# Linear attention and two feed-forwards: converting the second down projection's rows in the second feed-forward

## The chip, the cores and the metric

The program runs on one core of one Trainium2 chip. The metric is the device time of one execution in microseconds. A core has five engines that run their own instruction queues and wait for each other by semaphores: TensorE (PE: matmuls; PEld: its weight loads), VectorE (DVE), ScalarE (ACT), GpSimd (POOL) and SyncE (SP), which here issues nearly all DMAs.

## The reference

```python
def _attn_ref(q, k, v, g_norm):            # 4 x 8 heads x 576 x 64
    kv = np.einsum('bhsd,bhse->bhde', k, v)
    out = np.einsum('bhsd,bhde->bhse', q, kv)
    rms = np.sqrt(np.mean(out * out, axis=-1, keepdims=True) + 1e-06)
    return out / rms * g_norm
def _moe_ref(x, w_gate, w_val, w_out):     # 2304 x 512, d_ff 1536
    g = x @ w_gate
    return (g / (1 + np.exp(-g)) * (x @ w_val)) @ w_out
def _moe2_ref(x, w_in, w_out):             # d_ff 2048
    h = x @ w_in
    return (np.maximum(h, 0) + np.log1p(np.exp(-np.abs(h)))) @ w_out
```

The three are chained: `_moe2_ref(_moe_ref(_attn_ref(...)))`. The weights come as 64-bit floats, all else as 32-bit floats.

## The kernel before

**Precision.** Every operand of a feed-forward matmul is split into a high part in the fast 32-bit form (fp32r, a cast on ScalarE) and a low part (the difference, on GpSimd or VectorE); `mm3` makes three matmuls of a product: high x high, and the two mixed ones. A weight tile of 128 x 512 arrives as 64-bit floats and is converted by bit operations (`convert`): a scaled copy on ScalarE (L260), a shift and two merges on VectorE (L263, L264, L268). Then come the high part on ScalarE and the low part.

**Tokens.** The 2304 tokens are four tiles of 512 (t = 0 to 3) and one of 256 (t = 4, "B"). The first feed-forward loops over the 12 column blocks j of d_ff, and in each over the five tiles: gate and value products (pg, pv), silu and product on ScalarE and VectorE (s, u, split into uh and ul), and the down product py, which VectorE adds into yacc (L493). py is made of two units' tails woven into later units, and its PSUM tiles are three (pool `po`).

**The second feed-forward** makes its up products in 7 instead of 8 block products (a Strassen-like scheme): two column blocks of w2_in (a "pair", jp = 0 to 7) against two token tiles. A block of seven products, `quad`, has the steps p1, p5, p6, p2, p7, p3, p4 on the banks X, Y and Z; between them stand the down products pz of the pair before (`late`), which VectorE adds into zacc (L779). Products and sums become the tiles c11, c22, c12, c21; ScalarE makes their softplus and the high part gh (L679, L680), GpSimd the low part gl (L681). The first pass (n = 0) takes token tiles 0 and 1 through all eight pairs, the second (n = 1) tiles 2 and 3, with the small tile B woven in (`rest`).

**Its operands** are made ahead. In the first feed-forward `pair2` converts a pair of w2_in column blocks (zi), makes four sums of them (s, L551) and the two row blocks of w2_out (zp), splits all six into kh and kl, and writes them to DRAM (w2d); `load2` brings them back, once in each pass. For the tokens, `block_steps` makes seven blocks b of yacc and of sums of yacc (L622), each with a high half on ScalarE (L605) and a low half (L609) on the engine that `BLO` names: for the first pass in the last turn j = 11 (`blocks1`), for the second in the last block of the first pass (`blocks2`).

**The order** is written out by the program itself: TensorE's steps are emitted in a fixed order, each advances a nominal clock by 0.216 us a matmul of 512 columns, and `defer(dt, f)` puts all other work into a heap that is emptied as that clock passes. STEP2 is the distance of a pair's steps on it, PAIR2 that of the pairs. Each engine runs what it got in the order in which it was emitted; tiles come from pools of a fixed number of buffers, and a tile waits for the last reader of the buffer that it takes over. The pool `stage` (5 buffers) holds raw weights and the first two column tiles wh of a pair.

Of the kernel before, what the change touches and what calls it, by code (L numbers as in the profile page):

```python
# [68 lines left out]
def tile_linear_attention_two_ffn(  # L69
# [411 lines left out]
    def ffn1_o(j, t):  # L481
        w = widths[t]

        def step(d):
# [15 lines left out]
            if j == F1 - 1 and t == B:  # L500
                if d == 0:
                    x_tiles(t, "y")
                defer(ADD1, part)
# [112 lines left out]

    def t_sum(n, o, a, b):
        def f():  # L620
# [4 lines left out]
    def half(n, i):
        return lambda: halves(n)[i]

    def block_steps(n, tags):

        return [  # L630
            block(n, 0, tags[0], half(n, 0)),
            t_sum(n, 0, 2, 0) + block(n, 1, tags[1], half(n, 0)),
            t_sum(n, 0, 3, 0) + block(n, 2, tags[2], half(n, 0)),
            block(n, 3, tags[3], half(n, 1)),
            t_sum(n, 2, 3, 2) + block(n, 4, tags[4], half(n, 2)),
            block(n, 5, tags[5], half(n, 3)),
            t_sum(n, 1, 1, 0) + block(n, 6, tags[6], half(n, 1)),
        ]
# [4 lines left out]
    def spread(steps, at, every):  # L643
        return [(at + every * i, f) for i, f in enumerate(steps)]

    def blocks1(t):

        if t == 1:
            s = block_steps(0, TAGS1)
            blk["steps"] = s  # L650
            return spread(s[0] + s[3], 0.5, 1.0)
        s = blk["steps"]
# [8 lines left out]
    def blocks2():
        s = block_steps(1, TAGS2)
        r = spread(s[0], 0.2, 0.6)
        for i in range(1, 7):
            r += spread(s[i], 1.4 + 2.4 * (i - 1), 0.75)
        return r
# [320 lines left out]
```

## Time and profile before

| | |
|---|---|
| median of 3 runs | 936.11 us (934.92 to 938.82) |
| profiled execution | 934.92 us, span 933.1 us |
| granted clock, mean over the span | 0.992 |
| PE, PEld busy | 890.3 us (95%), 741.4 us (79%) |
| DVE, ACT, POOL busy | 557.0, 335.6, 253.8 us (60, 36, 27%) |
| moved by DMA | 130.8 MB, mean 140 GB/s |

In the trace, attention and the first two turns of the first feed-forward take until about 150 us, the other turns until about 546 us, the first pass of the second feed-forward until about 700 us, the second pass until about 906 us, and then come the last down products and stores. A row of a timeline gives the start, the duration, the engine, the line and the instruction with the tile written <- tiles read; in brackets stands how long the engine was idle before it, and what ended that. Matmuls overlap: a busy TensorE has a matmul of 512 columns begin every 0.227 us.

### The profile page before, as it was taken

What the parts mean: (1) busy time and instruction counts of PE and PEld (TensorE: products, weight loads), DVE (VectorE), ACT (ScalarE), POOL (GpSimd) and SP (SyncE); (2) the same over time, 40 slices, a digit from 0 to 9 for tenths busy, and PEclk for the clock granted to TensorE, in tenths of its full rate; (3) what the DMA queues carried; (4) which work ended last, traced back from release to release, by engine and by line L of the source; (5) the groups of instructions that cost most, each with busy time, mean ns of one, the idle gap of its engine ahead of it and who ended that gap; (6) DMA issues with size and microseconds to landing.
All of it is one profiled execution on the core that took longest, in us unless ns stands there. A gap on an engine that the chain in (4) does not pass through costs nothing.

```text
span 933.1 us, 11802 instructions
## 1 busy us (share of the span) xinstructions
PE 890.3 (95%) x4352; PEld 741.4 (79%) x4352; DVE 557.0 (60%) x874; ACT 335.6 (36%) x586; POOL 253.8 (27%) x197
## 2 busy tenths in 40 slices
PE   6889999999999999999999889999999999999994
PEld 5668888888888878888778778888877888888883
DVE  3955457988888778888896653333365333333332
ACT  3634434433334333333341352333344333332330
POOL 1633211414133222323131342222222322222220
PEclk9999999999999999999999999999999999999997
DMA  9975202344473636453536041544333543333102
GB/s 276 243 133 116 91 1 91 131 162 154 140 225 106 234 115 221 136 182 136 181 113 225 22 158 35 182 172 154 135 136 136 181 181 136 136 136 136 46 12 101
DMA packets 95453, 130.79 MB, mean 140 GB/s; under 512 B 28836, under 2 KB 57508, under 8 KB 95140
## 3 DMA queue, kind: packets, MB, share of 16 engines
q1 hardware_dynamic: 95236, 130.05, 42.8%
q8 instruction: 34, 0.56, 0.3%
q14 instruction: 23, 0.19, 0.1%
q10 hardware_dynamic: 160, 0.00, 0.0%
HBM read 100.14 MB, written 29.88 MB: 139 GB/s over the span
## 4 chain that ended last, share of the span: by engine, by line
PE 74%; DVE 18%; ACT 3%; issue 2%; DMA 1%; POOL 0%; SPq 0%; DVEq 0%; ACTq 0%; POOLq 0%
PE pz L433 20%; PE py L433 11%; PE pg L433 11%; PE pv L433 10%; PE hY L433 8%; PE hZ L433 4%; DVE yacc L493 4%; PE hX L433 2%; PE hr L433 2%; DVE ul L476 1%; DVE s L551 1%; ACT uh L475 1%; DVE u L472 1%; PE pa L363 1%; PE kvp L315 1%
## 5 line engine op out<-in xcount | busy, mean ns | idle before, releaser
L779 DVE TENSOR_TENSOR zacc<-zacc,pz 128x512 f32<-128x512 f32 x126 | 86.4, 687 | 160.5 <-PE pz L433 160.5
L433 PE MATMUL pz<-wo,gh 128*128 128x512 f32 x576 | 178.0, 390 | 1.1 <-ACT c L679 1.1
L493 DVE TENSOR_TENSOR yacc<-yacc,py 128x512 f32<-128x512 f32 (+1 forms) x220 | 133.3, 626 | 24.9 <-PE py L433 24.6
L681 POOL TENSOR_TENSOR gl<-c,gh 128x512 fp32r<-128x512 f32 x64 | 82.6, 1293 | 234.0 <-ACT gh L680 191.4
L433 PEld LDWEIGHTS pz<-wo,gh 128*128 128x128 f32 x576 | 106.8, 188 | 22.4 <-ACT c L679 1.5
L433 PE MATMUL pz<-wo,gl 128*128 128x512 f32 x288 | 112.3, 390 | 0.3 <-POOL gl L681 0.3
L433 PE MATMUL py<-uh,oh 128*128 128x512 f32 (+1 forms) x240 | 91.3, 380 | 11.3 <-DVE yacc L493 9.5
L433 PE MATMUL hY<-b,wh 128*128 128x512 f32 x384 | 97.6, 390 | 1.2 <-DVE c L709 1.2
L475 ACT CAST uh<-u 128x512 fp32r<-128x512 f32 (+1 forms) x60 | 34.7, 578 | 158.0 <-DVE u L472 157.9
L433 PE MATMUL pv<-xh,vh 128*128 128x512 f32 (+1 forms) x240 | 90.1, 376 | 0.0
L433 PE MATMUL pg<-xh,gh 128*128 128x512 f32 (+1 forms) x240 | 90.0, 375 | 0.0
L433 PE MATMUL pg<-xl,gh 128*128 128x512 f32 (+1 forms) x240 | 88.6, 369 | 0.5 <-DVE xl L401 0.5
L433 PE MATMUL py<-ul,oh 128*128 128x512 f32 (+1 forms) x240 | 88.6, 369 | 0.3 <-DVE ul L476 0.3
L433 PE MATMUL pv<-xh,vl 128*128 128x512 f32 (+1 forms) x240 | 88.8, 370 | 0.0
L433 PE MATMUL py<-uh,ol 128*128 128x512 f32 (+1 forms) x240 | 88.7, 370 | 0.0
L433 PE MATMUL pv<-xl,vh 128*128 128x512 f32 (+1 forms) x240 | 88.6, 369 | 0.0
L433 PE MATMUL pg<-xh,gl 128*128 128x512 f32 (+1 forms) x240 | 88.5, 369 | 0.0
L433 PEld LDWEIGHTS hY<-b,wh 128*128 128x128 f32 x384 | 71.6, 188 | 16.2 <-DVE c L709 1.7
L476 DVE TENSOR_TENSOR ul<-u,uh 128x512 fp32r<-128x512 f32 (+1 forms) x60 | 43.9, 732 | 39.2 <-ACT uh L475 39.2
L433 PEld LDWEIGHTS py<-uh,oh 128*128 128x128 f32 x240 | 45.2, 188 | 24.6 <-DVE yacc L493 15.1
L433 PEld LDWEIGHTS pz<-wo,gl 128*128 128x128 f32 x288 | 54.1, 188 | 12.6 <-POOL gl L681 1.2
L679 ACT ACTIVATE c<-c 128x512 f32<-128x512 f32 x48 | 30.3, 632 | 87.8 <-DVE c L709 87.7
(109 smaller groups left out, 1481.2 us busy)
## 6 DMA issues: line engine op xcount, KB each, us to landing
wh<-w2d SPq DMA_DIRECT2D x32, 512.0 KB, 6.5
wh<-w2d SPq DMA_DIRECT2D x64, 256.0 KB, 7.1
wo<-w2d SPq DMA_DIRECT2D x64, 256.0 KB, 3.7
w2d<-kh SPq DMA_DIRECT2D x48, 256.0 KB, 2.3
w2d<-kl SPq DMA_DIRECT2D x48, 256.0 KB, 2.4
ir<-in_moe_w_in_dram SPq DMA_DIRECT2D x16, 512.0 KB, 5.6
pr<-in_moe_w_out_dram SPq DMA_DIRECT2D x16, 512.0 KB, 3.8
gr<-in_moe_w_gate_dram SPq DMA_DIRECT2D x12, 512.0 KB, 4.5
```

Source lines behind the costliest of these rows:

```text
L315: nc.tensor.matmul(pk[:, hp, :], lhsT=kt[:, c, i:i + 2, :].rearrange("p h d -> p (h d)"), rhs=vt[:, i:i + 2, c * D:(c + 1) * D], start=(c ...
L363: nc.tensor.matmul(pv[p0:p0 + n, hp, :], lhsT=qt[:, hp, p0:p0 + n], rhs=kvm[bb][:, hp, :], start=True, stop=True,)
L433: nc.tensor.matmul(dst, lhsT=a, rhs=b_, start=first and i == 0, stop=last and i == n - 1, skip_group_check=not check)
L472: nc.vector.tensor_mul(u, s[0], pv)
L475: nc.scalar.copy(uh, u)
L476: (nc.gpsimd if UL1 == "g" else nc.vector).tensor_sub(ul, u, f32(uh))
L493: defer(ADD1, lambda: nc.vector.tensor_add(a[:, d, :], a[:, d, :], p))
L551: (nc.vector.tensor_sub if op == "-" else nc.vector.tensor_add)(o, a, b)
L679: nc.scalar.activation(l, src, AF.Softplus)
L681: nc.gpsimd.tensor_sub(lo, l, f32(hi))
L779: defer(ADD2, lambda: nc.vector.tensor_add(av[:, m, :], av[:, m, :], p))
```

## The change

- The row blocks of w2_out are no longer converted in the first feed-forward, nor written to DRAM and loaded twice. `load_rows2` loads the two raw row blocks of a pair into `stage` tiles, and `rows2` converts and splits them into the tiles from which pz reads: in both passes, in the block of the same pair (one block ahead of their use), from 5.0 on the nominal clock and 1.1 apart. The first pair's are loaded two turns before the end of the first feed-forward and converted at the start of its last turn.
- STEP2 becomes 2.05: a pair in `pair2` has 18 steps instead of 28.
- `load2(0)` is called two token tiles later.
- The blocks b: for the first pass, the second sum goes to a tile t2 of its own (from `stage`), so it no longer overwrites what the low half of b1 reads; the fourth sum (n4) is made of it earlier; other low halves go to GpSimd and VectorE. For the second pass they are spread over the last two blocks of the first pass and the first of the second; b0's parts and two sums come in the last block but one, and two low halves go to GpSimd.
- The small tile's y is split in one piece of 1024 columns (ScalarE, GpSimd) instead of four of 256 (ScalarE, VectorE).

```diff
-STEP2 = 1.35
+STEP2 = 2.05
+Q = 19.4
+ROWS2 = 5.0
+ROWS2_STEP = 1.1
-BLO = ["ggvgggv", "vvvvvvv"]
+BLO = ["gvggggv", "gvvgvvv"]
...
-            def part():
-                yh, yl = xt["y", t]
-                nc.scalar.copy(yh[:, d, :], a[:, d, :])
-                nc.vector.tensor_sub(yl[:, d, :], a[:, d, :], f32(yh[:, d, :]))
+            def high():
+                nc.scalar.copy(xt["y", t][0], a)
+
+            def low():
+                nc.gpsimd.tensor_sub(xt["y", t][1], a, f32(xt["y", t][0]))
...
-        steps += conv("p", 0) + kept(4, ("p", 0)) + conv("p", 1) + kept(5, ("p", 1))
         for k_ in range(2):
             defer(at - LOAD2 + 1.0 * k_, lambda k_=k_: load_cols(w2_in, "i", js[k_]))
-            defer(at + 10.0 + 6.0 * k_, lambda k_=k_: load_rows(w2_out, "p", js[k_]))
...
+    def load_rows2(jp):
         for i in range(2):
-            hl = [wop.tile([P, DM], F32R, tag="o" + "hl"[k_], name=f"wo{jp}_{i}{k_}") for k_ in range(2)]
-            for k_ in range(2):
-                nc.sync.dma_start(f32(hl[k_]), w2d[jp][4 + i][:, k_, :])
-            w2["o", jp, i] = hl
+            load_rows(w2_out, "p", 2 * jp + i)
+
+    def rows2(jp, at):
+
+        for i in range(2):
+            def go(j=2 * jp + i):
+                for k_, f in enumerate(split_rows("p", j)):
+                    defer(ROWS2_STEP * k_, f)
+
+            wt.pop(("p", 2 * jp + i), None)
+            defer(at + 5 * ROWS2_STEP * i, go)
...
+        src = [0, 0, "t2" if n == 0 else 0, 1, 2, 3, 1]
+        parts_ = [block(n, f"b{i}", tags[i], lambda i=i: part(n, src[i])) for i in range(7)]
...
+        s["t1"] = t_sum(n, 0, 2, 0)
+        s["t2"] = t_sum(n, "t2", 3, 0, stage) if n == 0 else t_sum(n, 0, 3, 0)
+        s["t3"] = t_sum(n, 2, 3, 2)
+        s["n4"] = t_sum(n, 1, 1, src[2])
...
         if t == B:
-            return spread(s[1] + s[2], 0.5, 1.0)
+            at(0, t1=0.3, t2=1.0, t1h=2.0, t2h=3.0, t1l=3.5, t2l=4.0)
         if t == 2:
-            return spread(s[4] + s[5], 0.2, 0.9)
+            at(0, t3=0.2, b22h=0.8, n4=1.4, t3h=2.2, t3l=2.6, b22l=3.0)
...
+        at(1, b11h=2.0, b11l=3.0, t1=8.0, t3=12.0)
+        at(1, t1h=Q + 1.6, t1l=Q + 2.7, t2=Q + 4.0, t2h=Q + 5.4, t2l=Q + 6.5, b21h=Q + 7.5, b21l=Q + 8.5,
+           t3h=Q + 10.4, t3l=Q + 11.4, b22h=Q + 14.0, b22l=Q + 15.0, n4=Q + 17.0, n4h=Q + 20.0, n4l=Q + 21.0)
...
+            if j == F1 - 3:
+                defer(25.0, lambda: load_rows2(0))
...
-        load2(0)
+        rows2(0, 1.0)
...
         last(1, among(h[1], o[0]))
+        load2(0)
         last(B, h[B] + o[1])
...
+                if (n, jp) != (0, 0):
+                    defer(0.3, lambda jp=jp: load_rows2(jp))
+                    rows2(jp, ROWS2)
                 main = quad(jp, t0, t1)
-                if n == 0 and jp == F2 // 2 - 1:
-                    for dt, f in blocks2():
-                        defer(dt, f)
+                if n == 0 and jp == F2 // 2 - 2:
+                    blocks2()
```

Three places show how the instructions move. First VectorE in the turn j = 10 of the first feed-forward, between the down products of tiles 0 and 1; yacc0 and yacc1 are their accumulators, oz11 the next turn's w_out rows, zp14 a row block of w2_out. Before:

```order
L493 TENSOR_TENSOR yacc0_783<-yacc0_783,py10_0_3_4609 128x512
L263 TENSOR_SCALAR oz11_4625<-oz11_4625 128x512
L264 SCALAR_TENSOR_TENSOR oz11_4625<-or11_4510,oz11_4625 128x512
L263 TENSOR_SCALAR zp14_4637<-zp14_4637 128x512
L264 SCALAR_TENSOR_TENSOR zp14_4637<-pr14_4483,zp14_4637 128x512
L493 TENSOR_TENSOR yacc1_1010<-yacc1_1010,py10_1_0_4647 128x512
L268 SCALAR_TENSOR_TENSOR oz11_4625<-or11_4510,oz11_4625 128x512
L268 SCALAR_TENSOR_TENSOR zp14_4637<-pr14_4483,zp14_4637 128x512
L493 TENSOR_TENSOR yacc1_1010<-yacc1_1010,py10_1_1_4657 128x512
```

After:

```order
L496 TENSOR_TENSOR yacc0_767<-yacc0_767,py10_0_3_4391 128x512
L266 TENSOR_SCALAR oz11_4409<-oz11_4409 128x512
L267 SCALAR_TENSOR_TENSOR oz11_4409<-or11_4307,oz11_4409 128x512
L496 TENSOR_TENSOR yacc1_994<-yacc1_994,py10_1_0_4431 128x512
L271 SCALAR_TENSOR_TENSOR oz11_4409<-or11_4307,oz11_4409 128x512
L496 TENSOR_TENSOR yacc1_994<-yacc1_994,py10_1_1_4439 128x512
```

The three zp instructions are gone from between the adds that empty py's banks.

Second, VectorE in the hand-over, turn j = 11, from the last adds of tile 1 on; L622 (after: L639) is a sum of two halves of yacc, b0_2 and b1_0 low halves of blocks, yl4 the low part of the small tile. Before:

```order
L493 TENSOR_TENSOR yacc1_1010<-yacc1_1010,py11_1_3_4961 128x512
L622 TENSOR_TENSOR yacc0_783<-yacc1_1010,yacc0_783 128x1024 x2
L493 TENSOR_TENSOR yacc4_1436<-yacc4_1436,py11_4_0_4990 128x256
L498 TENSOR_TENSOR yl4_4996<-yacc4_1436,yh4_4995 128x256
L493 TENSOR_TENSOR yacc4_1436<-yacc4_1436,py11_4_1_5003 128x256
L498 TENSOR_TENSOR yl4_4996<-yacc4_1436,yh4_4995 128x256
L609 TENSOR_TENSOR b0_2_5007<-yacc0_783,b0_2_5007 128x1024
L493 TENSOR_TENSOR yacc4_1436<-yacc4_1436,py11_4_2_5015 128x256
L498 TENSOR_TENSOR yl4_4996<-yacc4_1436,yh4_4995 128x256
L472 TENSOR_TENSOR u11_2_5026<-s11_2_4984,pv11_2_4986 128x512
```

After:

```order
L639 TENSOR_TENSOR yacc0_767<-yacc1_994,yacc0_767 128x1024
L496 TENSOR_TENSOR yacc1_994<-yacc1_994,py11_1_3_4751 128x512
L639 TENSOR_TENSOR t2_0_4765<-yacc1_994,yacc0_767 128x1024
L620 TENSOR_TENSOR b1_0_4773<-yacc0_767,b1_0_4773 128x1024
L496 TENSOR_TENSOR yacc4_1420<-yacc4_1420,py11_4_0_4783 128x256
L496 TENSOR_TENSOR yacc4_1420<-yacc4_1420,py11_4_1_4793 128x256
L496 TENSOR_TENSOR yacc4_1420<-yacc4_1420,py11_4_2_4801 128x256
L475 TENSOR_TENSOR u11_2_4809<-s11_2_4775,pv11_2_4777 128x512
```

The second sum writes t2 instead of yacc0, and the yl instructions have left VectorE.

Third, VectorE in the fourth block of the first pass (jp = 3), from c11's add to c12's (c113_0, c223_0 and c123_0 are the tiles c11, c22, c12 of pair 3, pass 0; pz7 in the rows after is a row block of w2_out in conversion, pz2_... the down products). Before:

```order
L709 TENSOR_TENSOR c113_0_5679<-p13_0_5629,hX3_0_5671 128x512
L779 TENSOR_TENSOR zacc1_5288<-zacc1_5288,pz2_1_3_5686 128x512
L709 TENSOR_TENSOR c223_0_5700<-p53_0_5646,hY3_0_5621 128x512
L779 TENSOR_TENSOR zacc0_5365<-zacc0_5365,pz2_0_0_5707 128x512
L709 TENSOR_TENSOR c123_0_5721<-u23_0_5662,hZ3_0_5638 128x512
```

After:

```order
L726 TENSOR_TENSOR c113_0_5488<-p13_0_5430,hX3_0_5479 128x512
L796 TENSOR_TENSOR zacc1_5061<-zacc1_5061,pz2_1_3_5495 128x512
L726 TENSOR_TENSOR c223_0_5514<-p53_0_5447,hY3_0_5418 128x512
L266 TENSOR_SCALAR pz7_5512<-pz7_5512 128x512
L267 SCALAR_TENSOR_TENSOR pz7_5512<-pr7_5428,pz7_5512 128x512
L796 TENSOR_TENSOR zacc0_5151<-zacc0_5151,pz2_0_0_5521 128x512
L271 SCALAR_TENSOR_TENSOR pz7_5512<-pr7_5428,pz7_5512 128x512
L726 TENSOR_TENSOR c123_0_5538<-u23_0_5469,hZ3_0_5439 128x512
```

Three instructions of the second row's conversion stand between the adds for c22 and c12.

## Rows read from the trace of the kernel before

**Rows 1.** busy time by stage: stretch, its length, engines' busy us, clock, DMA, GB/s

```profile
150.00:515.00 365.00, 358.21 (x1733) 300.00 (x1733) 304.20 (x497) 130.47 (x237) 101.96 (x76) 1.00 0.47 160
515.00:560.00 45.00, 39.84 (x190) 31.42 (x189) 26.00 (x38) 20.68 (x34) 19.00 (x11) 1.00 0.28 94
560.00:680.00 120.00, 120.00 (x531) 99.33 (x530) 45.23 (x66) 39.20 (x64) 29.41 (x23) 1.00 0.38 132
680.00:710.00 30.00, 27.69 (x120) 22.01 (x119) 22.81 (x25) 14.64 (x22) 6.77 (x6) 1.00 0.46 158
710.00:906.00 196.00, 196.00 (x944) 165.25 (x943) 68.07 (x99) 63.41 (x114) 50.73 (x45) 1.00 0.34 121
```

**Rows 2.** TensorE's waits, 150 to 515 us: us, times, longest

```profile
PE py L433 <- DVE yacc L493: 6.8, 11, 1.6
```

**Rows 3.** TensorE's waits, 515 to 560 us

```profile
PE py L433 <- DVE yacc L493: 2.7, 4, 1.4
PE py L433 <- ACT uh L475: 1.8, 1, 1.8
```

**Rows 4.** TensorE's timeline at one wait: start, us, instruction, idle before

```profile
339.76 0.28 PE L433 MATMUL pv<-xl,vh 128*128 128x256 f32 x1
341.60 0.50 PE L433 MATMUL py<-uh,oh 128*128 128x512 f32 x1 [1.56 <-DVE yacc L493]
341.94 0.40 PE L433 MATMUL py<-uh,ol 128*128 128x512 f32 x1
```

**Rows 5.** row conversions zp, 150 to 515 us: busy by engine

```profile
150.00:515.00 365.00, 31.82 (x48) 20.57 (x32) 21.89 (x16) 1.00 0.47 160
```

**Rows 6.** one tile's instructions, zi: ns min/median/max, first and last start

```profile
L263 DVE TENSOR_SCALAR zi<-zi x16: 418/422/1064, 153.5 to 462.6; 128x512 int32<-128x512 int32 x16
L264 DVE SCALAR_TENSOR_TENSOR zi<-ir,zi x16: 691/692/1668, 153.9 to 463.0; 128x512 int32<-128x512 int32 x16
L268 DVE SCALAR_TENSOR_TENSOR zi<-ir,zi x16: 677/684/693, 154.7 to 465.9; 128x512 int32<-128x512 int32 x16
```

**Rows 7.** VectorE's timeline in a pair's sums

```profile
163.93 0.42 DVE L551 TENSOR_TENSOR s<-zi,zi 128x256 f32<-128x256 f32 x1
164.26 1.52 DVE L551 TENSOR_TENSOR s<-zi 128x256 f32<-128x256 f32 x1
```

**Rows 8.** GpSimd's timeline beside it

```profile
164.14 1.36 POOL L282 TENSOR_TENSOR gl<-gz,gh 128x512 fp32r<-128x512 f32 x1 [13.76 <-ACT gh L279]
```

**Rows 9.** VectorE's timeline in the hand-over

```profile
525.34 1.23 DVE L622 TENSOR_TENSOR yacc<-yacc,yacc 128x1024 f32<-128x1024 f32 x1 [3.59 <-POOL b L609]
...
527.37 0.42 DVE L498 TENSOR_TENSOR yl<-yacc,yh 128x256 fp32r<-128x256 f32 x1 [0.47 <-ACT yh L497]
...
538.90 2.81 DVE L476 TENSOR_TENSOR ul<-u,uh 128x512 fp32r<-128x512 f32 x1 [0.69 <-ACT uh L475]
```

**Rows 10.** GpSimd's timeline in the hand-over

```profile
522.91 2.40 POOL L609 TENSOR_TENSOR b<-yacc,b 128x1024 fp32r<-128x1024 f32 x1 [2.42 <-ACT b L605]
```

**Rows 11.** groups by line and form, ScalarE: count, busy us, mean ns, idle before

```profile
L605 ACT CAST b<-yacc 128x1024 fp32r<-128x1024 f32 x14 | 14.5, 1048 | 12.9 <-DVE yacc L622 12.8
```

**Rows 12.** TensorE's timeline, a block of the first pass begins

```profile
661.60 1.52 PE L433 MATMUL hY<-b,wh 128*128 128x512 f32 x6
662.96 0.62 PE L433 MATMUL pz<-wo,gh 128*128 128x512 f32 x2
```

**Rows 13.** VectorE's timeline, the block before it

```profile
653.73 0.69 DVE L709 TENSOR_TENSOR c<-p,hY 128x512 f32<-128x512 f32 x1 [0.77 <-PE hY L433]
...
656.45 0.69 DVE L709 TENSOR_TENSOR c<-u,hZ 128x512 f32<-128x512 f32 x1 [0.77 <-PE hZ L433]
```

**Rows 14.** GpSimd's timeline, the same block

```profile
658.59 1.29 POOL L681 TENSOR_TENSOR gl<-c,gh 128x512 fp32r<-128x512 f32 x1 [1.48 <-issue]
```

**Rows 15.** DMA issues: instruction, count, KB each, median us to landing

```profile
pr<-in_moe_w_out_dram SPq DMA_DIRECT2D x16, 512.0 KB, 3.8
```

**Rows 16.** one line's instructions, L779: ns min/median/max

```profile
L779 DVE TENSOR_TENSOR zacc<-zacc,pz x126: 673/687/690, 582.9 to 919.6; 128x512 f32<-128x512 f32 x126
```

More of the change, by code (lines that the diff above doesn't have):

```diff
@@ L62 @@
 YL = "gggg"
-WLO2 = "gggggg"
-BLO = ["ggvgggv", "vvvvvvv"]
+WLO2 = "gggg"
+BLO = ["gvggggv", "gvvgvvv"]
 GLO = "gggg"
@@ L493, in step @@
                 defer(ADD1, lambda: nc.vector.tensor_add(a[:, d, :], a[:, d, :], p))
-            def part():
-                yh, yl = xt["y", t]
-                nc.scalar.copy(yh[:, d, :], a[:, d, :])
-                nc.vector.tensor_sub(yl[:, d, :], a[:, d, :], f32(yh[:, d, :]))
[L500 to L503, printed above, removed]
+            def high():
+                nc.scalar.copy(xt["y", t][0], a)
+            def low():
+                nc.gpsimd.tensor_sub(xt["y", t][1], a, f32(xt["y", t][0]))
+            if j == F1 - 1 and t == B and d == KD - 1:
+                x_tiles(t, "y")
+                defer(ADD1, high)
+                defer(ADD1, low)
         return [lambda d=d: step(d) for d in range(KD)]
     KH = KD // 2
-    w2d = [[dram.tile([P, 2, DM], F32, name=f"w2d{jp}_{i}") for i in range(6)] for jp in range(F2 // 2)]
+    w2d = [[dram.tile([P, 2, DM], F32, name=f"w2d{jp}_{i}") for i in range(4)] for jp in range(F2 // 2)]
     def pair2(jp, at):
@@ L602, in hi @@
         def hi():
-            t = xp.tile([P, 2, KH, T], F32R, tag=tag, name=f"b{n}_{i}")
+            t = xp.tile([P, 2, KH, T], F32R, tag=tag, name=f"{i}_{n}")
             blk[n, i] = t
@@ L625, in half, with part @@
-    def half(n, i):
-        return lambda: halves(n)[i]
-    def block_steps(n, tags):
[L630 to L638, printed above, removed]
+    def part(n, i):
+        if (n, i) in blk:
+            return blk[n, i]
+        a = acc["y", 2 * n + i // 2]
+        return a[:, KH * (i % 2):KH * (i % 2 + 1)]
@@ new lines, in t_sum @@
+    def t_sum(n, o, a, b, place=None):
+        def f():
+            x, y = part(n, a), part(n, b)
+            if place is None:
+                dst = part(n, o)
+            else:
+                dst = place.tile([P, KH, T], F32, tag="stage", name=f"t2_{n}")
+            nc.vector.tensor_sub(dst, x, y)
+            blk[n, o] = dst
+        return f
+    def block_steps(n, tags):
+        src = [0, 0, "t2" if n == 0 else 0, 1, 2, 3, 1]
+        parts_ = [block(n, f"b{i}", tags[i], lambda i=i: part(n, src[i])) for i in range(7)]
+        s = {}
+        for nm, p in zip(("b11", "t1", "t2", "b21", "t3", "b22", "n4"), parts_):
+            s[nm + "h"], s[nm + "l"] = p
+        s["t1"] = t_sum(n, 0, 2, 0)
+        s["t2"] = t_sum(n, "t2", 3, 0, stage) if n == 0 else t_sum(n, 0, 3, 0)
+        s["t3"] = t_sum(n, 2, 3, 2)
+        s["n4"] = t_sum(n, 1, 1, src[2])
+        return s
@@ L640, in tile_linear_attention_two_ffn, with at @@
     TAGS1 = ["xh0", "xl0", "xh1", "xl1", "xh2", "xl2", "xh3"]
     TAGS2 = ["xl3"] + TAGS1[:6]
-    def spread(steps, at, every):
-        return [(at + every * i, f) for i, f in enumerate(steps)]
+    blks = {}
+    def at(n, **when):
+        for nm, dt in when.items():
+            defer(dt, blks[n][nm])
     def blocks1(t):
         if t == 1:
[L649 to L652, printed above, removed]
+            blks[0] = block_steps(0, TAGS1)
+            at(0, b11h=0.5, b11l=1.0, b21h=2.0, b21l=2.5)
@@ L653, in blocks1 @@
         if t == B:
-            return spread(s[1] + s[2], 0.5, 1.0)
+            at(0, t1=0.3, t2=1.0, t1h=2.0, t2h=3.0, t1l=3.5, t2l=4.0)
         if t == 2:
-            return spread(s[4] + s[5], 0.2, 0.9)
+            at(0, t3=0.2, b22h=0.8, n4=1.4, t3h=2.2, t3l=2.6, b22l=3.0)
         if t == 3:
-            return spread(s[6], 0.2, 0.9)
-        return []
+            at(0, n4h=0.2, n4l=1.2)
     def blocks2():
[L662 to L665, printed above, removed]
@@ L772, in step @@
             mm3(p, [
-                (tuple(g[:, m * P:(m + 1) * P] for g in gs[k_]), w2["o", jp, k_])
+                (tuple(g[:, m * P:(m + 1) * P] for g in gs[k_][0]), gs[k_][1])
                 for k_ in range(2)
@@ L920, in last @@
                 f()
-            if t:
-                for dt, f in blocks1(t):
-                    defer(dt, f)
+            blocks1(t)
         last(0, among(h[0], behind[0] + behind[1]))
         last(1, among(h[1], o[0]))
+        load2(0)
         last(B, h[B] + o[1])
```

16 lines of the change are left out of this document (4 added, 12 removed).

## The prediction

> **What bounds the kernel now.** I read the busy time by stage first, then TensorE's waits, then the timelines around the waits. TensorE issues the same matmuls in the same order in both kernels, so only the time in which it stands still can change. By stage [rows 1], it is busy 358.2 of 365 us in the first feed-forward, 39.8 of 45 us in the hand-over to the second, all of 120 us in the first pass of the second, 27.7 of 30 us where the first pass meets the second, and all of 196 us after that. The granted clock is 1.00 throughout (the 2.4 GHz level), so the clock is no term. In the first feed-forward all waiting is one kind: py waits for VectorE's yacc add to empty its bank, 6.8 us in 11 waits [rows 2]. In the hand-over it is the same wait, 2.7 us in 4, and one wait of 1.8 us for ScalarE's uh [rows 3].
>
> A wait costs more than its figure. The wait of 1.56 us [rows 4] puts the next matmul 1.84 us behind the last one, where 256 columns take 0.12, and the one after follows after 0.34 instead of 0.23: 1.83 us in all, 0.27 above the figure. So the first feed-forward loses 6.8 + 11 x 0.27 = 9.8 us, the hand-over (45 - 39.84 = 5.16 us, some 7 waits) 7.0 us, the meeting of the passes (2.31 us, 2 waits) 2.8 us. At most 19.6 us can be won there, and the two full stretches can only lose.
>
> **First feed-forward.** The 16 conversions of w2_out rows leave it: 48 VectorE instructions of 31.8 us, 32 on ScalarE of 20.6 and 16 on GpSimd of 21.9 [rows 5], with 16 loads and 32 writes to DRAM that nothing on TensorE's chain waits for; in the second, 64 loads of 256 KB become 32 of 512 KB, counting the first pair's two still in the first. VectorE goes from 304.2 to 272.4 us of 365 [rows 1], 83 to 75%. The steps of a pair then stand 2.05 apart instead of 1.35: a conversion of w2_in columns (0.42 + 0.69 + 0.68 = 1.79 us on VectorE, [rows 6]) asks for 1.79/6.15 = 29% of it while it lasts instead of 1.79/4.05 = 44%; on top of an average of 83% the second is an overload and queues up, on top of 75% the first barely is. Also fewer VectorE instructions meet GpSimd: a sum of 256 columns took 0.42 us, the next 1.52, since a GpSimd subtraction had just begun [rows 7, 8]. Lower bound: only the waits go that have a row conversion right ahead of them; I count one of the long ones, some 2 us. Upper bound: all 9.8. Between them I take 60%, 5.9 us, since the load falls by a tenth and the bursts by a third.
>
> **Hand-over.** Before, the second block sum stands in VectorE's queue until GpSimd has read the first: it idles 3.59 us [rows 9] behind a subtraction of 2.40 us [rows 10], and the yacc adds that TensorE needs are queued behind it. After, that sum goes to a tile of its own, so nothing there waits for GpSimd. Four small yl subtractions, each with a wait for ScalarE (0.47 us in the row shown, [rows 9]) ahead of 0.42 us, leave VectorE: 3.6 us less in its queue. GpSimd gets one yl of 1024 columns instead, 2.4 us by its neighbours [rows 10]; ScalarE's yh, a cast of 1024 columns of 1.05 us [rows 11], and it end some 3.5 us behind the last yacc add, and 20 matmuls of 0.227 us, 4.5 us, lie between that add and the hr matmul that reads yl: hidden by about 1 us. The same walk puts ul beside two GpSimd subtractions again, as where it took 2.81 us [rows 9]; so some of the last waits stay. I leave 2.0 of the 7.0 us: a gain of 5.0, bounds 2 and 7.
>
> The row conversions of the first pair now stand in the last turn of the first feed-forward, where VectorE has none of the next weights to convert; the loads go to SP ahead of the first columns. I price that at nothing, with 0.5 us at worst.
>
> **Second feed-forward, first pass.** Each block of seven products now has two row conversions: on VectorE 2 x 1.79 us, on ScalarE 4 and on GpSimd 2 instructions, in 15 steps of six matmuls at 1.36 us [rows 12], 20.4 us. The engines have room (VectorE 45 of 120 us busy, [rows 1]), so the price is in the order: the second row's three instructions stand in VectorE's queue ahead of the add for c12, whose gh and gl are wanted by the first pz of the next block. Before: the c22 add at 653.73, the c12 add at 656.45 [rows 13], its gl at 658.59 to 659.88 [rows 14]; gl is wanted by the third matmul of the next block's pz, at 662.96 + 2 x 0.227 = 663.41 [rows 12]. Margin 3.5 us. After, and free of meetings: the second raw row's load is released by the end of p6, the fifth step of a block that began 20.4 us before 661.60: 648.0; it lands 3.8 us later [rows 15], 651.8, before ScalarE comes to it, about 653, behind c11's add, softplus and cast that follow the seventh step (650.7). From the c22 add's end at 654.4: shift 0.42, merge 0.69, zacc 0.69, merge 0.68, c12 add to 657.6, 0.45 us later than now. Then gl ends at 660.3 and the row's own pl, behind it on GpSimd, at 661.6; pl is wanted at 663.87, two matmuls behind gl. Margin 2.2 us: price 0.
>
> With meetings: GpSimd has the first row's pl from 654.4 to 655.7, behind c11's gl, and gl of c22 from 655.9 to 657.1, 2.1 us behind its add as c12's is [rows 13, 14]. The shift is held to 655.7 and the merge to 657.1; c12 ends at 659.9, gl at 662.6, pl at 663.9, just late: 0.1 + 0.27 us per block, for 7 blocks 2.6 us. The adds that read PSUM are not held: zacc took 673 to 690 ns in all 126 cases [rows 16]. So 0 to 2.6; I take 1.0.
>
> The Trainium skill bears on this meeting: by it ("SBUF — State Buffer", section "Who interferes with whom") a VectorE instruction with two inputs in SBUF and a GpSimd instruction that reads SBUF exclude each other, whichever starts second blocks to the end of the first, and one with a single SBUF input outside the two-port modes is not touched. The trace agrees: 1.52 against 0.42 us where both inputs are in SBUF, never a stretched zacc. By that rule the term is 2.6 us, without it 0; it speaks against adding such conversions beside GpSimd's work.
>
> In the second pass a block is 26 us for the same chain, so the margin is over 5 us larger: 0.
>
> **Where the passes meet.** Before, VectorE has in one block 8 zacc, 3 adds, 7 lows and 4 sums: 11 x 0.69 + 11 x 1.22 = 21.0 us of 20.4, and p4 waits. After: 11 x 0.69, two rows (3.6), 4 lows and 2 sums (7.3): 18.5 us; the rest moved a block earlier, into the next, or to GpSimd. But lows of 2.4 us on GpSimd now meet the row conversions, and the bank that p4 wants is again emptied by the c22 add, which stands behind the b4 low: my walk gives anything from no wait to 4 us. I take no change, bounds -2.8 and +2.5.
>
> **The sum** from the profiled execution's 934.9 us (span 933.1 and 1.8 around it): -5.9 - 5.0 + 1.0 + 0 = 925.0. The median of the runs shown stands 1.2 us above that execution: 926.2.
>
> **The rivals.**
> A: the waits hang on the columns' bursts and the sums, not on the rows, and the passes' meeting gets worse: -2 - 2 + 2.6 + 2.5 = +1.1, or with half of that -2: 933 to 937 us. For it: most long waits have w2_in or first-feed-forward conversions ahead of them. Against: those bursts are stretched too.
> B, slower: in the first pass the row conversions meet GpSimd more often than in my walk. Place: the first pz of the blocks 2 to 8. Each further hold is one GpSimd subtraction, 1.3 us [rows 14]. One more hold: 7 x (1.4 + 0.27) = 11.7 us, 936.9 in all, no change; two more: 7 x 2.97 = 20.8, 934.9 - 10.9 + 20.8 + 1.2 = 946 us. It decides from 2.2 us per block. For it: the margin is gone in the walk with meetings. Against: it needs all three instructions held in most blocks, and a pl behind gl each time.
> C: everything is won: -9.8 - 7.0 - 2.8 = 915.3, 916.5 us.
> D: the raw row lands late. Its load is released only by p6; at 7.1 us instead of 3.8 ScalarE would hold c22 behind it by 2.3 us, and the chain is at B's first step: 930 to 937, in A's and the forecast's range.
>
> **How the numbers follow.** My forecast (920 to 931) has 0.62, C 0.08, A with D's worse half 0.22, B 0.08. The range 918 to 935 leaves out B, the upper end of A and half of C. This kernel's measurement tells 0.5%, 4.7 us, from no change: below 931.4 is faster (0.62 + 0.08 + a little of A = 0.71), above 940.8 slower (0.08), the rest 0.21.
>
> **What would show it.** In the first feed-forward py's waits for yacc fall from 6.8 to about 2.5 us, with VectorE near 272 us. In the hand-over the idle time behind GpSimd's b is gone and TensorE idles under 2 us. In the first pass TensorE stays at 120 of 120 us, or waits under 0.4 us at the first pz of a block for pl or gl; if those waits are 1.5 us or more, seven times, B holds. I am wrong if py's waits stay above 5 us, or if a new wait stands in every block.

## The result and the profile after

After: 920.92 us median of 4 runs (920.24 to 923.55); the kernel before on the same chip 936.64 (934.92 to 938.82). The ratio is 0.984, 95% interval [0.981, 0.987]: faster. The time is inside the range, 5.3 us below the predicted 926.2. The profiled execution took 920.24 us, span 918.5, against 934.92 and 933.1.

TensorE issues its matmuls in the same order in both kernels, so the two traces can be lined up matmul by matmul, and the lag of one behind the other read at any place. Its steps by stage:

| stage (us of before) | forecast | measured |
|---|---|---|
| up to 150, where nothing was changed | 0 | -1.2 |
| first feed-forward, 150 to 515 | -5.9 | -9.7 |
| hand-over, 515 to 556 | -5.0 | -5.3 |
| first pass, its seven blocks | +1.0 | 0.0 |
| start of the eighth block, the passes' meeting, to 712 | 0 | +1.5 |
| second pass and end | 0 | 0.0 |
| sum | -9.9 | -14.7 |

The first row of the table is no work of the change: it is TensorE's clock, which fell for 3.4 us in attention in the profile of the kernel before and not in this one (last section). In a second profile of the changed kernel, where it fell too, the row was 0.0, and all other rows were the same within 0.1. So the change itself won 13.5 us of the 14.7.

The busy time by stage of the kernel after, the stages shifted with its lag (columns as in [rows 1]):

```profile
150.00:505.00 355.00, 354.59 (x1732) 299.88 (x1731) 267.38 (x455) 114.69 (x207) 80.53 (x62) 1.00 0.34 116
505.00:545.00 40.00, 38.79 (x189) 31.87 (x188) 23.41 (x32) 19.70 (x30) 22.03 (x12) 1.00 0.27 92
545.00:665.00 120.00, 120.00 (x531) 99.38 (x530) 74.84 (x103) 51.05 (x85) 48.38 (x34) 1.00 0.44 151
665.00:696.00 31.00, 27.91 (x118) 21.33 (x117) 26.41 (x28) 18.81 (x29) 15.81 (x10) 1.00 0.39 130
696.00:892.00 196.00, 196.00 (x944) 165.26 (x943) 105.18 (x147) 81.29 (x146) 75.58 (x61) 1.00 0.34 116
```

TensorE is full in the first feed-forward now, where it stood still for 6.8 of 365 us [rows 1]; VectorE has fallen from 83 to 75% there and risen from 45 to 75 of 120 us in the first pass, where TensorE still doesn't wait. Its waits, from 150 us on (total, times, longest), answer to [rows 2, 3]:

```profile
PE py L436 <- DVE yacc L496: 1.3, 3, 0.7
PE pz L436 <- POOL pl L285: 2.0, 2, 1.5
PE hY L436 <- DVE c L726: 0.9, 1, 0.9
PE pz L436 <- POOL gl L698: 0.6, 2, 0.3
```

Of py's three waits one, of 0.4 us, is in the first feed-forward, where there were 11 of 6.8 us [rows 2]; the wait for uh [rows 3] is gone. The waits for pl and c, and the shorter of the two for gl, are where the passes meet. TensorE's timeline at three of them:

```profile
684.21 1.65 PE L436 MATMUL hY<-b,wh 128*128 128x512 f32 x6 [0.88 <-DVE c L726]
690.81 0.50 PE L436 MATMUL pz<-ph,gl 128*128 128x512 f32 x1 [0.22 <-POOL gl L698]
693.02 0.50 PE L436 MATMUL pz<-pl,gh 128*128 128x512 f32 x1 [1.48 <-POOL pl L285]
```

And VectorE and GpSimd ahead of them:

```profile
682.08 1.47 DVE L620 TENSOR_TENSOR b<-yacc,b 128x1024 fp32r<-128x1024 f32 x1 [1.71 <-ACT b L616]
683.48 0.67 DVE L726 TENSOR_TENSOR c<-p,hY 128x512 f32<-128x512 f32 x1
...
689.67 2.17 DVE L639 TENSOR_TENSOR yacc<-yacc 128x1024 f32<-128x1024 f32 x1
```

```profile
689.47 1.28 POOL L698 TENSOR_TENSOR gl<-c,gh 128x512 fp32r<-128x512 f32 x1 [2.60 <-ACT gh L697]
690.71 2.26 POOL L285 TENSOR_TENSOR pl<-pz,ph 128x512 fp32r<-128x512 f32 x1
```

The add for c22 stands behind the low half of b4, as the prediction feared. At 690 us three instructions met: the sum of 1024 columns began 0.2 us behind gl and took 2.17 us instead of 1.23, and pl, which began while the sum ran, 2.26 instead of 1.3.

In an ordinary block of the first pass two of the second row's three conversions are held, as in the walk with meetings, though it is the two merges and not the shift. GpSimd and VectorE in the third block:

```profile
597.43 1.48 POOL L285 TENSOR_TENSOR pl<-pz,ph 128x512 fp32r<-128x512 f32 x1
598.87 1.75 POOL L698 TENSOR_TENSOR gl<-c,gh 128x512 fp32r<-128x512 f32 x1
...
604.41 1.30 POOL L285 TENSOR_TENSOR pl<-pz,ph 128x512 fp32r<-128x512 f32 x1
```

```profile
597.79 1.67 DVE L267 SCALAR_TENSOR_TENSOR pz<-pr,pz 128x512 int32<-128x512 int32 x1
...
599.98 1.18 DVE L271 SCALAR_TENSOR_TENSOR pz<-pr,pz 128x512 int32<-128x512 int32 x1
601.09 0.68 DVE L726 TENSOR_TENSOR c<-u,hZ 128x512 f32<-128x512 f32 x1
```

The second row's pl ends at 605.71; the block's fifth pz matmul, the first to read it, starts at 606.87. The slack is 1.2 us, between the 2.2 and -0.1 of the prediction's two walks. Rival D did not come about: between 545 and 665 us the raw rows landed 3.1 to 4.9 us behind their issue, and ScalarE waited for them twice, 0.5 us in all.

In the seventh block a sum for the second pass stands between the c22 add and those conversions (VectorE), and the next block's first pz waits 0.50 us for pl (TensorE):

```profile
658.45 1.57 DVE L639 TENSOR_TENSOR yacc<-yacc 128x1024 f32<-128x1024 f32 x1
```

```profile
668.98 0.50 PE L436 MATMUL pz<-pl,gh 128*128 128x512 f32 x1 [0.50 <-POOL pl L285]
```

### The profile page after: what moved, and what is told of

It is laid out like the page before. It is cut to its first block, busy times and chain, and to the rows that moved or that the text cites. A ratio compares the mean times of both kernels' runs of the same rounds, so it can differ in the third digit from the quotient of the medians.

```text
span 918.5 us, 11708 instructions
## 1 busy us (share of the span) xinstructions
PE 885.1 (96%) x4352; PEld 740.8 (81%) x4352; DVE 588.8 (64%) x916; ACT 353.1 (38%) x615; POOL 288.4 (31%) x216
## 4 chain that ended last, share of the span: by engine, by line
PE 83%; DVE 6%; issue 3%; SPq 2%; POOL 2%; ACT 1%; DMA 1%; POOLq 0%; DVEq 0%; ACTq 0%
PE pz L436 20%; PE pv L436 15%; PE pg L436 15%; PE py L436 15%; PE hY L436 8%; PE hZ L436 4%; PE hr L436 2%; PE hX L436 2%; PE pa L366 1%; POOL b L620 1%; DMA qr<-in_q_dram 1%; PE kvp L318 1%; SPq L181 1%; DVE yacc L496 1%; POOL gl L698 1%
## 5 line engine op out<-in xcount | busy, mean ns | idle before, releaser
L496 DVE TENSOR_TENSOR yacc<-yacc,py 128x512 f32<-128x512 f32 (+1 forms) x220 | 136.4, 629 | 53.6 <-PE py L436 53.0
L698 POOL TENSOR_TENSOR gl<-c,gh 128x512 fp32r<-128x512 f32 x64 | 88.5, 1383 | 189.7 <-ACT gh L697 145.4
L436 PE MATMUL pz<-pl,gh 128*128 128x512 f32 x288 | 112.5, 391 | 2.0 <-POOL pl L285 2.0
L436 PE MATMUL pz<-ph,gl 128*128 128x512 f32 x288 | 112.4, 390 | 0.6 <-POOL gl L698 0.6
L436 PE MATMUL pz<-ph,gh 128*128 128x512 f32 x288 | 112.4, 390 | 0.0
L436 PEld LDWEIGHTS pz<-pl,gh 128*128 128x128 f32 x288 | 54.2, 188 | 13.2 <-POOL pl L285 2.9
L436 PEld LDWEIGHTS pz<-ph,gl 128*128 128x128 f32 x288 | 54.1, 188 | 13.0 <-POOL gl L698 1.8
L479 DVE TENSOR_TENSOR ul<-u,uh 128x512 fp32r<-128x512 f32 (+1 forms) x60 | 38.8, 647 | 39.1 <-ACT uh L478 39.1
L436 PEld LDWEIGHTS pz<-ph,gh 128*128 128x128 f32 x288 | 54.1, 188 | 10.9 <-ACT ph L282 0.3
```

Source lines behind the costliest of these rows:

```text
L436: nc.tensor.matmul(dst, lhsT=a, rhs=b_, start=first and i == 0, stop=last and i == n - 1, skip_group_check=not check)
L479: (nc.gpsimd if UL1 == "g" else nc.vector).tensor_sub(ul, u, f32(uh))
L496: defer(ADD1, lambda: nc.vector.tensor_add(a[:, d, :], a[:, d, :], p))
L698: nc.gpsimd.tensor_sub(lo, l, f32(hi))
```

## The experiments

Each change below is to the kernel named. Lags are read from the profiles as above, ratios are to the kernel before on the same chip.

**The pitch alone (e1).** The changed kernel with

```diff
-STEP2 = 2.05
+STEP2 = 1.35
```

> The changed kernel with one edit: the steps of a pair of w2_in columns stand 1.35 apart again instead of 2.05; the row conversions stay in the second feed-forward. Theory L (load: py's waits went because VectorE has a tenth less to do in the first feed-forward): py's waits for yacc between 150 and 505 us stay under 2 us (changed kernel 0.4, before 6.8), and the time stays within 2 us of the changed kernel's 921, 919 to 923 us. Theory P (pitch: they went because the pair's instructions stand further apart, 1.79 us on VectorE per 6.15 us instead of per 4.05): the waits come back to 4 to 7 us with 6 to 11 of them, and the time is 926 to 931 us. In both the hand-over and the second feed-forward are as in the changed kernel.

926.5 us, ratio 0.991 [0.989, 0.992]. The first feed-forward gains 3.7 us on the kernel before, not 9.7; the hand-over is the same, and the meeting loses 3.1 us, 1.6 of them to the clock (last section). Both theories hold in part: the load that left is worth 3.7, and the pitch on top of it 6.0. The queues show where most of the 3.7 come from. In the kernel before, two of py's eleven waits have instructions of a row among the five ahead of VectorE's add, those at 228 and 456 us, of 0.21 and 1.26 us; both are gone here, and the wait of [rows 4] fell from 1.56 to 0.75 us. Of the eleven, nine have a held instruction there, of the nine that are left here eight. The wait at 167.60 us of the kernel before follows the sum of [rows 7] and another held like it (VectorE, then TensorE):

```profile
165.71 1.51 DVE L551 TENSOR_TENSOR s<-zi,s 128x256 f32<-128x256 f32 x1
167.14 0.41 DVE L493 TENSOR_TENSOR yacc<-yacc,py 128x256 f32<-128x256 f32 x1
```

```profile
167.60 0.39 PE L433 MATMUL py<-uh,oh 128*128 128x256 f32 x1 [0.84 <-DVE yacc L493]
```

**The load alone (e2).** The changed kernel with the rows converted in the first feed-forward too:

```diff
-WLO2 = "gggg"
+WLO2 = "gggggg"
...
+        extra = conv("p", 0) + kept(4, ("p", 0)) + conv("p", 1) + kept(5, ("p", 1))
+        for k_ in range(2):
+            defer(at - 5.0 + 18.0 * k_, lambda k_=k_: load_rows(w2_out, "p", js[k_]))
+        for k_, f in enumerate(extra):
+            defer(at + 4.9 + 3.5 * k_, f)
```

> The changed kernel, with the conversions of the 16 w2_out row blocks put into the first feed-forward once more (48 VectorE, 32 ScalarE, 16 GpSimd instructions, their loads and writes to DRAM; what they write is never read), beside the pair's own steps, which stay 2.05 apart. Theory L: VectorE is at 300 us of 355 there again, py's waits for yacc come back to 4 to 7 us, and the time is 926 to 931 us. Theory P: the waits stay under 2 us and the time within 2 us of 921. If both load and pitch carry a part, this run and the one with the old pitch each show 2 to 4 us of waits.

935.2 us, 0.999 [0.998, 1.001]. The first feed-forward loses 5.1 us more than the kernel before, 1.2 of them to the clock (last section); that is worse than either theory, or both in part, had expected. So here the wide pitch gained nothing without the room that the rows left: 18 steps at 2.05 fill the 40 us of a pair that 28 at 1.35 filled, and two chains at once, with the rows 3.5 apart beside the columns, were worse than one.

**The two halves of the change apart (e3, e4).** The kernel before with the new hand-over alone (t2, order and engines of the first blocks, y in one piece):

> The kernel before, with the change in the hand-over alone: the second sum goes to a tile t2, the new order of the blocks of the first pass and their new engines, y of the small tile in one piece on ScalarE and GpSimd, the first pair's load two token tiles later. The rows are converted in the first feed-forward, 1.35 apart, and the second pass's blocks are made as before. By the theory that the terms stand apart: 5 us less than the kernel before run beside it (931 to 932 where it is 936.6), TensorE busy 38.5 of the 40 us of the hand-over, py's waits between 150 and 515 us unchanged at 6 to 8 us. Rival: the hand-over is better only because VectorE comes to it without a queue of row conversions; then under 2 us less, and waits of 3 us or more stay in the hand-over.

929.4 us, 0.994 [0.992, 0.995]; the hand-over gains 5.4 us, the first feed-forward 0.1. And the changed kernel with the old hand-over:

> The changed kernel with the old hand-over: the second sum in place again, the old order and engines of the blocks of the first pass, y of the small tile in four pieces on ScalarE and VectorE, the first pair's load two token tiles earlier. If the terms stand apart: 5 us more than the changed kernel (925 to 927 us), waits of 4.5 us (2.7 for yacc, 1.8 for uh) in the hand-over again, VectorE idle 3 us or more behind GpSimd's first b, py's waits before it under 1 us. Rival: the hand-over's waits came from the rows' load and not from the order; then within 2 us of the changed kernel's 921.

929.1 us, 0.992 [0.990, 0.994]; the first feed-forward gains 9.7 us, the hand-over loses 1.6. Its waits are those of [rows 3], to the tenth:

```profile
PE py L436 <- DVE yacc L496: 2.7, 4, 1.4
PE py L436 <- ACT uh L478: 1.8, 1, 1.8
```

So the terms stand apart, and the hand-over's waits come from the order there. (The 1.6 us beside them are nearly all the clock's, in the last section.)

**The changed kernel again (e5),** as the reference of the next three:

> The changed kernel once more, on the chip of the three runs below, as their reference: 920 to 923 us, 0.984 of the kernel before, waits of TensorE as in its first profile (some 0.5 us in the first feed-forward, 2 us in the hand-over, 3.1 us where the passes meet).

923.4 us, 0.985 [0.984, 0.987].

**GpSimd's holds or VectorE's load (e8, e9, e10).** In the first feed-forward a VectorE instruction counts here as held where it took over 0.1 us more than others of its form (0.42 us for 256 columns or a shift, 0.69 for 512); the time above that is summed. Three edits of the kernel before. Without GpSimd's low halves of the pairs:

```diff
-            lo = pages.tile([P, DM], F32R, tag="pg", name=f"kl{jp}_{i}")
-            (nc.gpsimd if WLO2[i] == "g" else nc.vector).tensor_sub(lo, src, f32(hi))
...
-            nc.sync.dma_start(w2d[jp][i][:, 1, :], f32(lo))
+            nc.sync.dma_start(w2d[jp][i][:, 1, :], f32(hi))
```

> The kernel before without the 48 GpSimd subtractions of its pairs in the first feed-forward (of four column results and two rows a pair; the high half is written to DRAM in their place, so the low halves of the second feed-forward's weights are left out of the result). VectorE's instructions are all there. Theory H (holds: py's bank is emptied late because VectorE's instructions ahead of the add are held by GpSimd, 41 of them stretched by 31.2 us in all in the kernel before): py's waits between 150 and 515 us fall from 6.8 to under 2.5 us, the stretching to under 15 us, and the time is 928 to 931 us. Theory O (occupancy: the instructions themselves, 300 of 365 us, make the queue): waits of 5 us or more and 934 us or more.

925.9 us, 0.988 [0.987, 0.990]. (The edit takes the tiles of these low halves away too, but the profile of the kernel before puts none of VectorE's waits there down to GpSimd or to a buffer that it holds.) Without VectorE's part of the row conversions:

```diff
-            return [lambda i=i: s(i) for i in range(3)]
+            return [lambda i=i: s(i) if nm == "i" or i == 0 else None for i in range(3)]
```

> The kernel before without the 48 VectorE instructions of its row conversions in the first feed-forward (the shift and the two merges; the scaled copy goes on as it is, so the down projection's weights are wrong), while GpSimd's 76 subtractions there all stay. This is the counterpart of the run without GpSimd's subtractions. Theory H (holds): VectorE falls to some 272 us as in the changed kernel, but only the 3.3 us of stretching that fell on the row conversions go (31.82 us against 48 instructions of 0.42 to 0.69 us, 28.5 us); 25 us or more stay, and the first feed-forward still loses 6 us or more of its 9.8: 932 to 936 us. Theory O (occupancy): the loss falls to 3 us or less, 928 to 930 us.

932.9 us, 0.996 [0.995, 0.998]. And with the low halves moved to VectorE:

```diff
-WLO2 = "gggggg"
+WLO2 = "vvvvvv"
```

> The kernel before with the 48 subtractions of its pairs (the low halves of four column results and two rows a pair) on VectorE instead of GpSimd: complete, nothing left out. VectorE gets 48 x 0.69 = 33 us more to do in the first feed-forward and no longer meets 48 of GpSimd's 76 subtractions. Theory H: its busy time grows by less than that, 304 to about 315 us, the stretching falls from 31 to under 10 us, and the first feed-forward loses under 5 us instead of 9.8, 931 us or less. Theory O: at 91% with bursts of steps 1.35 apart py's waits grow to 10 us or more, 937 to 945 us.

936.2 us, 1.000 [0.998, 1.001]. The first feed-forward in all of them:

| kernel | VectorE busy | held: instructions, us | lag gained or lost |
|---|---|---|---|
| before | 83% | 41, 31.2 | 0 |
| rows in the second feed-forward, pitch 1.35 (e1) | 77% | 30, 24.4 | -3.7 |
| after, pitch 2.05 | 75% | 15, 12.3 | -9.7 |
| after, rows beside it (e2) | 83% | 39, 32.0 | +5.1 |
| before, no GpSimd lows (e8) | 80% | 11, 7.9 | -8.6 |
| before, no row conversions on VectorE (e9) | 76% | 34, 26.2 | -3.6 |
| before, lows on VectorE (e10) | 85% | 19, 10.8 | +0.2 |

Their busy times (columns as in [rows 1]), e8, e9 and e10 in turn:

```profile
150.00:506.00 356.00, 354.98 (x1730) 299.74 (x1729) 283.53 (x497) 130.25 (x236) 36.62 (x28) 1.00 0.49 164
```

```profile
150.00:513.00 363.00, 358.76 (x1747) 301.53 (x1746) 277.09 (x451) 131.79 (x239) 102.32 (x76) 1.00 0.49 161
```

```profile
150.00:515.00 365.00, 358.14 (x1734) 299.86 (x1733) 311.54 (x545) 130.72 (x237) 39.43 (x28) 1.00 0.48 161
```

VectorE is busier in e8 than in e9, and TensorE waits less: occupancy as such is not the cause. Without a single VectorE instruction less, e8 wins nearly all. But the pure theory of holds falls too, at e10: 20 us of holds went, 33 us of VectorE's own work came in bursts of the same pitch, and nothing was won, where it had expected half. The simplest reading is that a held instruction and an additional one both lengthen the queue ahead of the add that empties py's bank; no run sets a price on the one against the other. The waits for that add in e9 are those of e1, nine of 4.2 us, longest 0.8, so of the rows' work it was VectorE's three instructions that counted, and what e9 leaves in, ScalarE's and GpSimd's part, the loads and the writes, nothing that shows. That the pitch's 6.0 us come through the 12 us of holds that went with it is likely by e8, but was not tried by itself.

The hold itself is seen at one form, the sums s; these are the 16 of 32 that read an earlier sum (ns min/median/max), first before, then e8, then after:

```profile
L551 DVE TENSOR_TENSOR s<-zi,s x16: 410/420/1512, 165.7 to 473.2; 128x256 f32<-128x256 f32 x16
```

```profile
L551 DVE TENSOR_TENSOR s<-zi,s x16: 411/418/426, 165.6 to 464.5; 128x256 f32<-128x256 f32 x16
```

```profile
L555 DVE TENSOR_TENSOR s<-zi,s x16: 409/418/1518, 169.7 to 468.3; 128x256 f32<-128x256 f32 x16
```

Without GpSimd's low halves none of these is held. Of the other 16 four are held in e8 as before, up to 1.52 us: one of them is the second sum of [rows 7], which stands beside a subtraction of the first feed-forward's weights [rows 8], and those e8 leaves in. After, one of the 32 is held: the longest is as long as before, but the sum of these 16 is 7.8 us instead of 10.4.

**The slack of the first pass (e6).** The changed kernel with each row's low half made twice:

```diff
...
-                for k_, f in enumerate(split_rows("p", j)):
+                fs = split_rows("p", j)
+                def again(j=j):
+                    nc.gpsimd.tensor_sub(wt["p", j][1], zs["p", j], f32(wt["p", j][0]))
+                for k_, f in enumerate(fs):
                     defer(ROWS2_STEP * k_, f)
+                if jp:
+                    defer(ROWS2_STEP * (len(fs) - 1), again)
```

> The changed kernel, in which GpSimd makes the low half pl of each row block twice in the second feed-forward (the same tile, the same values), from the second pair on: one GpSimd subtraction of 1.3 us more for each row. In the changed kernel's trace the second row's pl ends 0.5 us before the block's first pz reads it (605.7 against 606.2 us). If the slack of the first pass is this half microsecond: the second subtraction ends 0.8 us late, or 2.0 us if VectorE's conversion is held once more and c12 with it, with 0.27 beside each wait 1.1 to 2.3 us in each of six or seven blocks, 7 to 16 us in all, 928 to 937 us, with a wait of pz for pl in each block of the first pass and none in the second. If TensorE's stream has more slack than that in the first pass: waits under 2 us in all and under 923 us.

929.1 us, 0.992 [0.991, 0.993], against 0.985 of the changed kernel. The expectation took the wrong matmul: the second row's pl is read by the block's fifth, 1.2 us behind its end, not by the second. With 1.2 us, a subtraction of 1.3 us should cost 0.1, and so it did in three blocks (waits of 0.14, 0.08 and 0.08 us at 587, 608 and 651 us); in one, where VectorE's shift was held as well, 1.19 us. Against the changed kernel the first pass loses 2.7 us to 667 us, the meeting 6.5 (a wait of 3.8 us for pl and two falls of the clock among it), the second pass nothing. So 929 us lies in the expected 928 to 937 by chance: most of the loss is the meeting's. Rival B had the place right, but one more GpSimd instruction of 1.3 us in each block cost three of the first four about 0.1 us of wait, not the 1.4 that B set for each.

**The meeting, and a better version (e7, e11).** The changed kernel with the blocks of the second pass begun one block of products earlier:

```diff
-        at(1, b11h=2.0, b11l=3.0, t1=8.0, t3=12.0)
-        at(1, t1h=Q + 1.6, t1l=Q + 2.7, t2=Q + 4.0, t2h=Q + 5.4, t2l=Q + 6.5, b21h=Q + 7.5, b21l=Q + 8.5,
-           t3h=Q + 10.4, t3l=Q + 11.4, b22h=Q + 14.0, b22l=Q + 15.0, n4=Q + 17.0, n4h=Q + 20.0, n4l=Q + 21.0)
+        at(1, b11h=2.0, b11l=3.0, t1=Q + 0.8, t3=Q + 3.4)
+        r = 2 * Q
+        at(1, t1h=r + 1.6, t1l=r + 2.7, t2=r + 4.0, t2h=r + 5.4, t2l=r + 6.5, b21h=r + 7.5,
+           t3h=r + 12.5, b22h=r + 14.5, t3l=r + 16.6, b21l=r + 20.0, b22l=r + 21.5,
+           n4=r + 24.5, n4h=r + 26.0, n4l=r + 27.5)
...
-                if n == 0 and jp == F2 // 2 - 2:
+                if n == 0 and jp == F2 // 2 - 3:
```

> The changed kernel with the blocks of the second pass called one block of products earlier: the two sums in the last block but two to one, and the low half of b4 behind the c22 add instead of ahead of it. Theory: the waits of TensorE between 667 and 693 us (0.5 at the block's first pz for pl, 0.9 for c22, 1.7 for gl and pl) come from the order in VectorE's and GpSimd's queues there: 2.5 to 4.5 us less than the changed kernel, 916.5 to 918.5 us. Rival: the engines are full there (VectorE 26.4 of 31 us), so the waits only move: within 1 us of the changed kernel, waits of 2 us or more between 640 and 715 us.

916.7 us, 0.979 [0.978, 0.981], below the changed kernel's interval. Busy time of the stage of the meeting, where the changed kernel had 27.91 of 31 us:

```profile
665.00:696.00 31.00, 31.00 (x139) 25.67 (x138) 23.33 (x31) 18.01 (x27) 15.08 (x10) 1.00 0.44 148
```

The waits there are gone but for one of 0.26 us at 709; against the changed kernel the lag gains 4.7 us by 694 us and gives back 0.6. The engines were not too full; it was the order. Then one low half in the hand-over, also later (on top of e7). The expectation names 4.2 on the nominal clock; the run has 5.0, and the low half stands behind three yacc adds, not two:

```diff
-            at(0, n4h=0.2, n4l=1.2)
+            at(0, n4h=0.2, n4l=5.0)
```

> The version with the passes' meeting spread, with one edit in the hand-over: the last low half of the first pass's blocks stands behind two more yacc adds in VectorE's queue (4.2 instead of 1.2 on the nominal clock). In the changed kernel's trace it was held to 1.80 us there and the first of those adds cost TensorE 0.67 us (0.83 with what lies beside it). If nothing else waits for that low half: 0.8 us less in the hand-over, 916 us, no wait at 528 us. Rival: the first block of the first pass reads it and waits instead, 0 to 2 us more.

That low half in the changed kernel (VectorE):

```profile
527.22 1.80 DVE L620 TENSOR_TENSOR b<-yacc,b 128x1024 fp32r<-128x1024 f32 x1 [0.95 <-ACT b L616]
```

916.1 us, 0.980 [0.978, 0.982]. The wait of 0.67 us that e7 had at 529 us is gone, and with it 0.95 us of lag; no new wait came at the first block. The median cannot tell it from e7. By the profile this is the best version: all that TensorE still waits between 500 and 900 us is 0.8 us, in three waits.

## Why the prediction came out as it did

- **First feed-forward:** the step that failed in size is "between them I take 60%, 5.9 us, since the load falls by a tenth and the bursts by a third". It measured 9.7, nearly all of the upper bound of 9.8. Both parts were at work (load 3.7, pitch 6.0, by e1), but the loss did not shrink in proportion to the load. The waits of [rows 2] were 0.6 us on average; one hold adds 1.1 us (1.52 instead of 0.42, [rows 7]), and a merge takes 0.69 [rows 6]. One such instruction less ahead of the add is longer than the average wait. That this is why nearly all of it went is argued from these lengths and the queues of e1; setting them side by side would have put the estimate nearer the upper bound.
- **Hand-over:** right, 5.3 for 5.0, and by its own order, as e3 and e4 show. A rest stayed, as forecast, though not by ul: 0.95 us of it hung on a low half of the blocks, which took 1.80 us instead of 1.22 ahead of an add for py. In e11, where it stands later, that rest is gone.
- **First pass:** priced at +1.0 for seven blocks; six cost nothing. The walk with meetings was too strict by 1.3 us of slack. The seventh block's rows did cost 1.0 us, at the place named, the first pz of the next block, but because a sum of the second pass's blocks stands ahead of the conversions of the second row there, right behind the c22 add. e7, which puts the sums ahead of both rows and b0's halves a block earlier, has no wait there. That the seventh block alone cost the 1.0 us taken for all seven is chance.
- **Meeting:** taken as no change within -2.8 to +2.5; it was +0.5 beside that 1.0. The c22 add behind the b4 low was seen ahead. The old waits of 2.3 us there had been replaced, not removed.
- **Sum:** 926.2 - 3.8 (first feed-forward) - 0.3 + 0.5 (hand-over; first pass and meeting) - 1.2 (the clock in attention) - 0.5 (the median stands 0.7, not 1.2, above the profiled execution) = 920.9. (In rival A, -2 - 2 and half of +5.1 is -1.5, not -2; its range holds either.)

The Trainium skill's rule ("SBUF — State Buffer", section "Who interferes with whom") agrees with these runs. It lets the adds that have one input in SBUF go free, and after, too, none of zacc's was held, right beside conversions held to 1.67 and 1.18 us (ns min/median/max):

```profile
L796 DVE TENSOR_TENSOR zacc<-zacc,pz x126: 672/686/689, 566.7 to 904.9; 128x512 f32<-128x512 f32 x126
```

The 2.6 us that it would have made of the first pass did not come about: in six blocks the holds fell into slack and cost nothing, and in the seventh they cost 1.0, with a sum among them.

## What to carry to other kernels

Where an engine at 80% makes the bottleneck wait for tenths of a microsecond, set the length of each wait beside the instructions queued ahead of it: taking out one of that length can remove the wait whole. Here a tenth less load won 3.7 of 9.8 us, and with what was left spread over the room 9.7. Count an instruction that another engine holds with its held length, and after taking work out, spread what is left over the room. Work belongs in the stage whose queue still has slack at the place where it is read: in six blocks of the first pass such held conversions cost nothing.

## What the runs showed of the hardware beside this

The prediction said that the clock is no term. Between 150 and 900 us it was none in the profiles of before and after, but in those of six variants (e1, e2, e4, e6, e8, e10) TensorE's granted clock fell to 0.50 there, behind waits, for 3 to 4 us (in e6 twice, once for 7). TensorE in e4's hand-over, with the same waits as [rows 3]:

```profile
535.63 0.50 PE L436 MATMUL py<-uh,oh 128*128 128x512 f32 x1 [0.54 <-DVE yacc L496]
...
538.02 0.50 PE L436 MATMUL py<-uh,oh 128*128 128x512 f32 x1 [1.43 <-DVE yacc L496]
...
539.17 2.76 PE L436 MATMUL hY<-b,wh 128*128 128x512 f32 x6
541.73 1.58 PE L436 MATMUL hZ<-b,wh 128*128 128x512 f32 x6
```

Its granted clock in that stretch (third figure from the end):

```profile
538.70:541.70 3.00, 3.00 (x8) 2.31 (x7) 1.15 (x2) 0.00 (x0) 0.00 (x0) 0.50 0.00 0
```

Six matmuls took 2.76 us instead of 1.52 [rows 12]; the granted clock is 0.50, the 1.2 GHz level. Seven matmuls at 0.427 instead of 0.227 us are 1.4 us, nearly all of the 1.6 us that e4's hand-over lost against the kernel before. The kernel before made the same waits in the same places at a clock of 1.00:

```profile
545.88 0.50 PE L433 MATMUL py<-uh,oh 128*128 128x512 f32 x1 [1.43 <-DVE yacc L493]
...
546.69 1.53 PE L433 MATMUL hY<-b,wh 128*128 128x512 f32 x6
```

In attention it is the other way round, and this is the first row of the table by stage. The code is the same there; the same stretch in before, then in after:

```profile
58.90:62.20 3.30, 3.30 (x13) 2.73 (x11) 0.71 (x1) 0.00 (x0) 0.00 (x0) 0.50 0.00 0
```

```profile
58.90:62.20 3.30, 3.30 (x21) 2.76 (x20) 0.75 (x1) 0.31 (x1) 0.00 (x0) 1.00 0.00 0
```

TensorE began 21 matmuls there instead of 13. In the 3.8 us from 55 us on it had been busy 1.35 us in before and 0.97 in after. What decides between the two levels, these runs don't show; but in these profiles a wait of that kind carried the risk of another 1.2 us or more.
